# Agent attention with a squared-ReLU network on one Trainium2 core: the first batch's passes over 98 columns instead of 49, its small work in another order

## The chip, the cores and the metric

One Trainium2 chip, of which the kernel uses one core. A core has five engines with a queue each: PE (TensorE, the matrix unit), DVE (VectorE), ACT (ScalarE), POOL (GpSimd) and SP (SyncE), which here only starts transfers (DMAs). PE reads SBUF and writes PSUM. The metric is the device time of one execution in microseconds (us), lower is better; a kernel's time is the median of its runs.

## What is computed

Four batches of 12480 tokens with 128 channels, 49 agents per batch, and a two-layer network behind the attention:

```python
scale = 1.0 / np.sqrt(q.shape[-1])
def sm(a, b):
    s = scale * (a @ b.transpose(0, 2, 1))
    s = s - s.max(-1, keepdims=True)
    e = np.exp(s)
    return e / (e.sum(-1, keepdims=True) + 1e-09)
agent_v = sm(agents, k) @ v          # 49 x 128 per batch
attn = sm(q, agents) @ agent_v       # 12480 x 128 per batch
h = np.maximum(attn @ w_in, 0.0)     # d_ff = 2048
out = h * h @ w_out
```

The two weight matrices arrive in 64-bit floats; the kernel turns their bits into f32 numbers itself ("decode").

## The kernel before

The kernel doesn't form the attention's output. Per batch it forms `agent_v` (transposed: avT), multiplies it with w_in into a table aw of 49 rows and 2048 columns, and the first layer is then the softmaxed queries (49 wide) times that table. High and low parts keep the precision: aw_hi and aw_ex for the table, w and x for the queries.

**The first batch** is computed alone, ahead of everything else, with an order written out by hand: while `alone[0]` is true every instruction of an engine is issued behind the one before it in program order (`Ordered`, `queued`, lines 55 to 74). Its stages:

- *Keys.* 13 blocks, twelve of 1024 tokens (8 tiles of 128) and one of 192. `scores` (177) multiplies each tile, as the stationary operand, with the agents (49 columns moving) into a PSUM buffer h; ACT copies the scores to s, DVE takes the running maximum mx. An f32 matmul is two records ("passes") in the trace. In between, `make_w_in` (143) decodes parts of w_in: ACT forms t from raw, DVE runs five operations on t and rest (`decoded`, 124), POOL adds them into win.
- *Maximum.* `maxima` (195): m on DVE, a transpose on PE, its maximum, a diagonal dg, and a matmul with ones that broadcasts it, copied to mb.
- *Values.* Per block `whole_exps` (227): subtract mb (DVE and POOL take turns), exponential on ACT in place in s. `whole_values` (233): each tile of values, stationary, times 49 columns of s, all accumulated in one PSUM bank; POOL adds the exponentials into mx for the row sums. In between, `make_w_out` (147) decodes parts of w_out (t, wo_hi, wo_lo), and the first 960 queries are softmaxed step by step (`queries`, 326).
- *Sums and tables.* `whole_sums` (248): the row sums e1, their reciprocal rl and avT. `tables` (301): four matmuls win x avT of 512 columns; ACT writes aw_hi, DVE aw_lo (3 buffers), SP moves pieces of aw_lo into aw_hi and aw_ex.

**The feed-forward part** then runs over 52 groups of 960 queries, each 16 steps k of two halves j (loop at 517). `first` (376) makes h from w, x and the table; `hidden` (394): ACT relu r, DVE r times h (gg), ACT square g_hi, DVE or POOL the rest g_lo; `second` (419) multiplies with wo_hi and wo_lo into o, four steps later. PE, ACT and DVE keep program order there too. Beside it `queries` prepares the next group (started at c = 0, one step from c = 2 on), and `background` the next batch's keys, values and tables; both share one PSUM bank, psa. None of it is issued ahead of the first batch's last instruction on SP, ACT, DVE and POOL (`behind`).

PSUM buffers h: 3 (two banks each). Buffers of loaded keys and values in the first batch: 11; of raw weights: 8.

Of the kernel before, what the change touches and what calls it, by code (L numbers as in the profile page):

```python
# [9 lines left out]
F32 = mybir.dt.float32  # L10
# [4 lines left out]
AX = mybir.AxisListType  # L15
PSUM = bass.MemoryType.PSUM

P = 128
# [18 lines left out]
def agent_attention_relu2(ctx: ExitStack, tc: tile.TileContext, qT, kT, v, agT, w_in, w_out, outT):  # L37
    nc = tc.nc
    C, NTOK = qT.shape
    _, B, NA = agT.shape  # L40
# [21 lines left out]
    alone = [True]  # L62
# [11 lines left out]
    pe, act, dve, pool, sync = (Ordered(e) for e in (nc.tensor, nc.scalar, nc.vector, nc.gpsimd, nc.sync))  # L74
# [4 lines left out]
    small = ctx.enter_context(tc.tile_pool(name="small", bufs=1))  # L79
# [6 lines left out]
    ag = const.tile([C, B, NA], F32, name="ag")  # L86
# [75 lines left out]
    state = {}  # L162
# [7 lines left out]
    def load_values(b, i, pool, name):  # L170
        at, rows, nt = blocks[i]
        vt = pool.tile([P, KB], F32, name=name).rearrange("p (t c) -> p t c", c=C)
        src = v[b, at : at + rows * nt, :].rearrange("(p t) c -> p t c", p=rows)
        sync.dma_start(vt[:rows, :nt, :], src)
        return vt

    def scores(b, i, kt):
        st = state.setdefault(b, {"s": []})
        _, rows, nt = blocks[i]
        ps = bank()  # L180
        sv = ps[:rows, : nt * NA].rearrange("p (t a) -> p t a", a=NA)
        for t in range(nt):
            pe.matmul(sv[:, t, :], kt[:, t * rows : (t + 1) * rows], ag[:, b, :], start=True, stop=True)  # L183
        yield
        s = sp.tile([P, NT, NA], F32, name="s")
        act.copy(s[:rows, :nt, :], sv)
        if i == 0:
            st["mx"] = small.tile([P, NT, NA], F32, name="mx")
            dve.tensor_copy(st["mx"], sv)
        else:  # L190
            mx = st["mx"][:rows, :nt, :]
            dve.tensor_max(mx, mx, sv)
        st["s"].append(s)

    def maxima(b):
        st = state[b]
# [30 lines left out]
    def whole_exps(b, i, eng):  # L227
        _, rows, nt = blocks[i]
        e = state[b]["s"][i][:rows, :nt, :]
        less_maximum(b, i, e, eng)  # L230
        act.activation(e, e, AF.Exp, scale=scale)

    def whole_values(b, i, vt):
        st = state[b]
        _, rows, nt = blocks[i]
        e = st["s"][i][:rows, :nt, :]
        if i == 0:
            st["pv"] = bank()
        for t in range(nt):
            pe.matmul(  # L240
                st["pv"][:C, :NA], vt[:rows, t, :], e[:, t, :],
                start=(i == 0 and t == 0), stop=(i == NK - 1 and t == nt - 1),
            )
        if i > 0:
            es = st["mx"][:rows, :nt, :]
            pool.tensor_add(es, es if i > 1 else st["s"][0], e)

    def whole_sums(b):
        st = state[b]
        e1 = small.tile([P, 2, NA], F32, name="e1")  # L250
        for n in range(2):
            dve.reduce_sum(e1[:, n, :], st["mx"].rearrange("p t a -> p a t"), axis=AX.X)
        pz = bank()
        pe.matmul(pz[:K2, :1], e1.rearrange("p h a -> p (h a)"), ones[:, :1], start=True, stop=True)
        rl = st["rl"] = small.tile([K2, 1], F32, name="rl")
        dve.tensor_scalar_add(rl, pz[:K2, :1], 1e-9)
        dve.reciprocal(rl, rl)
        av = st["avT"] = small.tile([C, K2], F32, name="avT")
        act.copy(av[:, :NA], st["pv"][:C, :NA])
        dve.tensor_copy(av[:, NA:], st["pv"][:C, :NA])  # L260

    def values(b, i, vt):
        st = state[b]
# [37 lines left out]
    def tables(b):  # L301
        st = state[b]
        rl, av = st["rl"], st["avT"]
        hi = st["hi"] = aw.tile([P, FF], F32R, name="aw_hi")
        ex = st["lo"] = aw.tile([P, NCH // NQ, P], F32R, name="aw_ex")
        for n in range(FF // 512):
            yield
            cs = slice(n * 512, (n + 1) * 512)
            pw = bank()
            pe.matmul(pw[:K2, :], av, win[:, cs], start=True, stop=True)  # L310
            yield
            act.activation(hi[:K2, cs], pw[:K2, :], AF.Copy, scale=rl)
# [151 lines left out]
    def run(gen):  # L464
        for _ in gen:
            pass
# [6 lines left out]
        pe.matmul(idle[:, 0, :P], ones, ones, start=True, stop=True)  # L473

    with tc.tile_pool(name="pre", bufs=PRE) as pre, tc.tile_pool(name="dec", bufs=2) as dec:
        raws = {}
        kts, vts = [], []
        early = {i: i - 3 for i in range(3, 8)} | {9: 5, 11: 6}
        for i in range(NK):
            kts.append(load_keys(0, i, pre, "ahead"))  # L480
            if 1 <= i <= NW:
                raws[i - 1] = ask_w_in(dec, i - 1)
            if i == NK - 3:
                q0 = queries(0)
                next(q0)
            run(scores(0, i, kts[i]))
            if i in early:
                make_w_in(dec, early[i], raws.pop(early[i]))
        top = maxima(0)
        next(top)  # L490
        next(top)
        next(q0)
        run(top)
        for i in range(NK):
            if i == NW:
                make_w_in(dec, NW - 1, raws.pop(NW - 1))
            vts.append(load_values(0, i, pre, "ahead"))
            if 1 <= i <= NW:
                raws[NW + i - 1] = ask_w_out(dec, i - 1)
        for i in range(2):  # L500
            whole_exps(0, i, (pool, dve)[i % 2])
        for i in range(NK):
            if i + 2 < NK:
                whole_exps(0, i + 2, (pool, dve)[i % 2])
            whole_values(0, i, vts[i])
            next(q0, None)
            if 3 <= i < NW + 3:
                make_w_out(dec, i - 3, raws.pop(NW + i - 3))
        run(q0)
        whole_sums(0)  # L510
        run(tables(0))
    behind = [chain[eng] for eng in (nc.sync, nc.scalar, nc.vector, nc.gpsimd)]

    alone[0] = False
    ffn = ctx.enter_context(tc.tile_pool(name="ffn", bufs=4))
    todo = ahead = iter(())
    for k in range(total + LAG):
        if k < total:
            g, c = divmod(k, SLOTS)
            b, i = divmod(g, NB)  # L520
            if i == 0 and c == 0 and b + 1 < B:
                todo = background(b + 1)
                done = 0
            goal = (i * SLOTS + c + 1) * STEPS / (SPREAD * NB * SLOTS)
            while done < goal and step(todo):
                done += 1
            if c == 0 and g + 1 < B * NB:
                ahead = queries(g + 1)
                step(ahead)
            if c >= 2:  # L530
                step(ahead)
        if k % 2 == 0:
            hs = first(k) if k < total else ()
            if hs:
                hidden(k, hs[0])
            for n in range(2):
                if k + n >= LAG:
                    second(k + n - LAG)
            copied_out()
            if hs:  # L540
                hidden(k + 1, hs[1])
# [35 lines left out]
```

## Time and profile before

| | us |
|---|---|
| median of 3 runs | 2089.64 (2088.23 to 2092.76) |
| the profiled execution | 2089.47 |
| its span from first to last instruction | 2087.6 |
| warm-up matmuls, from the span's start | 0 to 6.13 |
| key matmuls | 6.13 to 43.45 |
| maximum | 43.45 to 55.59 |
| value matmuls | 55.59 to 102.00 |
| sums | 102.00 to 108.76 |
| table matmuls | 108.76 to 114.68 |

The page's first part, busy time and share of the span for each engine:

```profile
PE 2051.5 (98%) x10932; PEld 1621.5 (78%) x10932; DVE 1672.7 (80%) x1835; ACT 1775.2 (85%) x2100; POOL 1275.1 (61%) x1110
```

PE is busy 98% of the span, and PEld is its weight load, which overlaps. A busy PE need not be a fast one: the granted clock has a row of its own. A row of the timeline reads: start, length, engine, line, operation, out<-in, shapes, count, and in brackets the idle time before it with what ended it. L58 is the helper through which all ordered instructions go, so rows are told apart by their tiles. "ahead" are the loaded keys or values.

### The profile page before, as it was taken

To read this page: it belongs to the slowest core of one execution; us is meant where nothing else is said; L and a number is where in the kernel's file an instruction comes from. 1 tells how busy PE (TensorE), PEld (TensorE's weight loads), DVE (VectorE), ACT (ScalarE), POOL (GpSimd) and SP (SyncE) were. 2 spreads that over 40 slices of the span, in tenths; PEclk is the share of its full clock that TensorE was granted. 3 is DMA by queue.
4 is the path that set the end of the run, shared out by engine and by line. 5 is a ranking of instruction groups with operands and counts; after the bars stand their busy time and mean duration, and the time that the engine had idled before them with its cause. 6 is when DMAs were issued, how large, how long until landed. Compare 5 with 4: busy or idle time off the path is not lost. (4 is left out here: it accounts for less than half of the span.)

```text
span 2087.6 us, 31676 instructions
## 1 busy us (share of the span) xinstructions
PE 2051.5 (98%) x10932; PEld 1621.5 (78%) x10932; DVE 1672.7 (80%) x1835; ACT 1775.2 (85%) x2100; POOL 1275.1 (61%) x1110
## 2 busy tenths in 40 slices
PE   8889999999999999999999999999999999999999
PEld 8857777777778877777778877777777777777777
DVE  3465888889887788888887788888888888888887
ACT  1265899989888899999898889999889999989897
POOL 1643587766554477776555458777556565656565
PEclk6588999999999999999999999999999999999999
DMA  8132222121112212221112211221111111111100
GB/s 300 46 118 87 70 75 75 52 65 63 53 56 79 65 53 80 63 60 61 63 40 71 88 35 60 68 75 41 44 51 35 46 35 47 35 47 35 38 23 20
DMA packets 55943, 131.34 MB, mean 63 GB/s; under 512 B 6712, under 2 KB 35336, under 8 KB 55784
## 3 DMA queue, kind: packets, MB, share of 16 engines
q1 hardware_dynamic: 55784, 129.33, 19.3%
q8 instruction: 87, 1.43, 0.3%
q14 instruction: 72, 0.59, 0.1%
HBM read 80.97 MB, written 25.56 MB: 51 GB/s over the span
## 5 line engine op out<-in xcount | busy, mean ns | idle before, releaser
L407 POOL TENSOR_TENSOR g_lo<-gg,g_hi 128x480 fp32r<-128x480 f32 x832 | 999.1, 1222 | 711.2 <-DVE gg L58 457.5
L58 ACT ACTIVATE r<-h 128x960 f32<-128x960 f32 x832 | 800.7, 962 | 145.5 <-PE h L58 132.7
L58 ACT ACTIVATE g_hi<-r 128x960 fp32r<-128x960 f32 x832 | 837.5, 1007 | 34.8 <-PE o L58 1.0
L58 DVE TENSOR_TENSOR h<-r,h 128x960 f32<-128x960 f32 x416 | 482.5, 1160 | 156.7 <-ACT r L58 151.6
L58 DVE TENSOR_TENSOR gg<-r,h 128x960 f32<-128x960 f32 x416 | 478.0, 1149 | 85.4 <-ACT r L58 79.9
L58 PE MATMUL o<-g_hi,wo_hi 128*128 128x480 f32 x1664 | 539.2, 405 | 0.0
L58 DVE TENSOR_TENSOR g_lo<-h,g_hi 128x960 fp32r<-128x960 f32 x416 | 481.0, 1156 | 48.3 <-ACT g_hi L58 7.7
L58 PE MATMUL h<-w,aw_hi 128*128 128x480 f32 x1664 | 485.4, 398 | 10.7 <-DVE gg L58 7.7
L58 PE MATMUL o<-g_hi,wo_lo 128*128 128x480 f32 x1664 | 495.4, 379 | 0.0
L58 PE MATMUL o<-g_lo,wo_hi 128*128 128x480 f32 x1664 | 494.7, 378 | 0.0
L58 PEld LDWEIGHTS o<-g_hi,wo_hi 128*128 128x128 f32 x1664 | 280.9, 188 | 117.4 <-issue 69.5
L58 PEld LDWEIGHTS o<-g_hi,wo_lo 128*128 128x128 f32 x1664 | 313.3, 188 | 47.2
L58 PEld LDWEIGHTS o<-g_lo,wo_hi 128*128 128x128 f32 x1664 | 313.3, 188 | 46.7
L58 PEld LDWEIGHTS h<-w,aw_hi 128*128 128x128 f32 x1664 | 289.3, 190 | 59.3 <-DVE gg L58 20.3
L58 PE MATMUL h<-x,aw_ex 19*128 19x480 f32 x1664 | 207.9, 481 | 1.3 <-DMA x<-w 1.0
L58 PEld LDWEIGHTS h<-x,aw_ex 19*128 19x128 f32 x1664 | 81.6, 182 | 142.4 <-issue 138.1
L334 PEld LDWEIGHTS psa<-ag,qt 128*120 128x120 f32 x816 | 100.6, 184 | 6.5 <-issue 0.7
L58 DVE COPY ob<-o 128x480 f32<-128x480 f32 x104 | 68.2, 656 | 35.9 <-PE o L58 35.5
L334 PE MATMUL psa<-ag,qt 128*120 128x49 f32 x816 | 95.9, 261 | 0.0
L219 POOL TENSOR_TENSOR vs<-vt,vs 128x1024 fp32r<-128x1024 f32 (+1 forms) x39 | 81.6, 2094 | 12.6 <-ACT vs L217 12.3
L183 PEld LDWEIGHTS psa<-ag,kt 128*128 128x128 f32 (+1 forms) x588 | 76.4, 195 | 3.6
L183 PE MATMUL psa<-ag,kt 128*128 128x49 f32 (+1 forms) x588 | 72.7, 271 | 0.0
(112 smaller groups left out, 1069.0 us busy)
## 6 DMA issues: line engine op xcount, KB each, us to landing
qt<-in_qT SPq DMA_DIRECT2D x52, 480.0 KB
out_T<-ob SPq DMA_DIRECT2D x104, 240.0 KB
kt<-in_kT SPq DMA_DIRECT2D x36, 512.0 KB
vt<-in_v SPq DMA_DIRECT2D x36, 512.0 KB
x<-w SPq DMA_DIRECT2D x416, 35.6 KB
ahead<-in_kT SPq DMA_DIRECT2D x12, 512.0 KB
ahead<-in_v SPq DMA_DIRECT2D x12, 512.0 KB
w<-w SPq DMA_DIRECT2D x104, 56.2 KB
```

The source lines that it names most:

```text
L58: ins = issue(*args, **kw)
L183: pe.matmul(sv[:, t, :], kt[:, t * rows : (t + 1) * rows], ag[:, b, :], start=True, stop=True)
L219: eng.tensor_sub(out[:, :, n : n + w], x, out[:, :, :w].bitcast(F32))
L334: pe.matmul(sv[:, t, :], qt[:, t * TP : (t + 1) * TP], ag[:, b, :], start=True, stop=True)
L407: nc.gpsimd.tensor_sub(lo[:, n, :], gg[:, n, :], hi[:, n, :].bitcast(F32))
```

## The change

In the first batch, key and value matmuls move 98 columns. For keys these are the agents of batches 0 and 1 side by side, of which only the first 49 columns of the result are read (each result tile now takes 128 columns, four to a bank, in both banks of an h buffer). For values, the exponentials of two neighbouring tiles are moved together past each value tile; even tiles go to one bank and odd ones to the other, the matching 49 columns of both are added at the end. The other changes are of order:

- DVE's maximum comes ahead of ACT's copy of the same scores.
- The input weight parts are decoded behind key blocks 3, 4, 6, 7, 9, 10 and the first two value blocks; output parts 0 to 5 behind value blocks 3, 4, 6, 7, 9, 10; output parts 6 and 7 behind the tables.
- The queries' scores go ahead of the maximum's transpose; four matmuls of ones (`warm`) stand ahead of the broadcast.
- All subtractions are on DVE, three ahead; POOL's additions are issued ahead of the matmuls (`add_weights`); e1 is summed once and copied, ahead of the last value block.
- Values are loaded interleaved with the output weights, later ones between the value matmuls.
- The second group's queries start ahead of the tables, with their scores and first steps right behind, and go on at every step of the first group.

```diff
     def scores(b, i, kt):
...
+        if alone[0]:
+            h = ps_h.tile([P, 2, 512], F32, name="h")[:rows, :, :].rearrange("p h (t x) -> p h t x", x=P)
+            n = nt // 2
+            for t in range(nt):
+                out = h[:, t // n, t % n, : 2 * NA]
+                keys = kt[:, t * rows : (t + 1) * rows]
+                pe.matmul(out, keys, ag[:, :2, :].rearrange("c b a -> c (b a)"), start=True, stop=True)
+            sv = h[:, :, :n, :NA]
...
         yield
         s = sp.tile([P, NT, NA], F32, name="s")
-        act.copy(s[:rows, :nt, :], sv)
...
         if i == 0:
-            st["mx"] = small.tile([P, NT, NA], F32, name="mx")
-            dve.tensor_copy(st["mx"], sv)
+            dve.tensor_copy(mx, sv)
         else:
             dve.tensor_max(mx, mx, sv)
+        act.copy(s, sv)
...
         if i == 0:
-            st["pv"] = bank()
+            st["pv"] = ps_h.tile([P, 2, 512], F32, name="h")
         for t in range(nt):
+            pair = e[:, t - t % 2 : t - t % 2 + 2, :].rearrange("p t a -> p (t a)")
             pe.matmul(
-                st["pv"][:C, :NA], vt[:rows, t, :], e[:, t, :],
-                start=(i == 0 and t == 0), stop=(i == NK - 1 and t == nt - 1),
+                st["pv"][:C, t % 2, : 2 * NA], vt[:rows, t, :], pair,
+                start=(i == 0 and t < 2), stop=(i == NK - 1 and t >= nt - 2),
             )
+    def add_weights(b, i):
...
+            pool.tensor_add(es, es if i > 1 else st["s"][0], st["s"][i][:rows, :nt, :])
 
     def whole_sums(b):
...
-        for n in range(2):
-            dve.reduce_sum(e1[:, n, :], st["mx"].rearrange("p t a -> p a t"), axis=AX.X)
+        dve.reduce_sum(e1[:, 0, :], st["mx"].rearrange("p t a -> p a t"), axis=AX.X)
+        dve.tensor_copy(e1[:, 1, :], e1[:, 0, :])
+        yield
+        av = st["avT"] = small.tile([C, K2], F32, name="avT")
+        act.copy(av[:, :NA], st["pv"][:C, 0, :NA])
+        dve.tensor_add(av[:, :NA], av[:, :NA], st["pv"][:C, 1, NA : 2 * NA])
+        dve.tensor_copy(av[:, NA:], av[:, :NA])
...
+        def warm(n):
+            idle = bank()
+            for _ in range(n):
+                pe.matmul(idle[:, :P], ones, ones, start=True, stop=True)
...
+        between = {i: n for n, i in enumerate((3, 4, 6, 7, 9, 10))}
...
         top = maxima(0)
         next(top)
+        next(q0)
         next(top)
-        next(q0)
+        warm(2)
+        next(top)
+        warm(2)
         run(top)
+        for i in range(3):
+            whole_exps(0, i, dve)
+        for i in range(2):
+            add_weights(0, i)
+        between = {i: n for n, i in enumerate((0, 1, 3, 4, 6, 7, 9, 10))}
         for i in range(NK):
+            if i + 3 < NK:
+                whole_exps(0, i + 3, dve)
             if i + 2 < NK:
-                whole_exps(0, i + 2, (pool, dve)[i % 2])
+                add_weights(0, i + 2)
+            if i == NK - 1:
+                ends = whole_sums(0)
+                next(ends)
             whole_values(0, i, vts[i])
             next(q0, None)
...
         run(q0)
-        whole_sums(0)
+        run(ends)
+        ahead = queries(1)
+        next(ahead)
         run(tables(0))
+        next(ahead)
+        next(ahead)
+        for n in range(NW - 2, NW):
+            make_w_out(dec, n, raws.pop(NW + n))
...
-            if c == 0 and g + 1 < B * NB:
+            if c == 0 and 0 < g < B * NB - 1:
                 ahead = queries(g + 1)
                 step(ahead)
-            if c >= 2:
+            if c >= 2 or g == 0:
                 step(ahead)
```

What the change moves is seen in the order of the instructions on an engine. ACT's queue in the key stage, from the third key block on; "COPY s" copies a block's scores, "ACTIVATE t" is the first step of a decode. Before:

```order
L58 COPY s<-h 128x392 [waits PE_49] x4
L58 ACTIVATE t<-raw 128x256 [waits DMAHW3_49]
L58 COPY s<-h 128x392 [waits PE_49]
L58 ACTIVATE t<-raw 128x256 [waits DMAHW5_49]
L58 COPY s<-h 128x392 [waits PE_49]
```

And now:

```order
L58 COPY s<-h 128x392 [waits DVE_49] x4
L58 ACTIVATE t<-raw 128x256 [waits DMAHW3_49]
L58 COPY s<-h 128x392 [waits DVE_49]
L58 ACTIVATE t<-raw 128x256 [waits DMAHW5_49]
L58 COPY s<-h 128x392 [waits DVE_49] x2
```

The copy waits for DVE (its maximum of the same block) where it waited for PE, and t still stands behind the copy.

DVE's queue between the tables (aw_lo) and the first products of the feed-forward part (gg). Before:

```order
L58 TENSOR_REDUCE e_727<-mx 128x49 x2
L58 TENSOR_SCALAR rl<-h 98x1
L58 RECIPROCAL rl<-rl 98x1
L58 COPY avT<-h 128x49
L58 SCALAR_TENSOR_TENSOR aw_lo<-h,rl,aw_hi 49x512 x4
L58 TENSOR_TENSOR gg<-r,h 128x960
```

And now, where m, e and z belong to the second group's queries:

```order
L58 SCALAR_TENSOR_TENSOR aw_lo<-h,rl,aw_hi 49x512 x4
L58 TENSOR_REDUCE m<-h 120x8
L58 TENSOR_TENSOR e<-h,m 120x392
L58 TENSOR_SCALAR t<-t 128x256 x2
L58 SCALAR_TENSOR_TENSOR t<-raw,t 128x256
L58 TENSOR_SCALAR rest<-t 128x256
L58 SCALAR_TENSOR_TENSOR rest<-raw,rest 128x256
...
L362 TENSOR_REDUCE z<-e 120x8
L363 TENSOR_SCALAR z<-z 120x8
L364 RECIPROCAL z<-z 120x8
L58 TENSOR_TENSOR gg<-r,h 128x960
```

Two decodes (one of them is the "...") and the second queries' first steps came in between.

PE's queue where the second group begins; w_999 (now w_904) are that group's weights, "psa<-identr,pp" the transposes that make them. Before:

```order
L183 MATMUL psa<-ag,kt 128x49 x8
L356 MATMUL psa<-identr,pp 98x120 x8
L58 MATMUL h<-w_999,aw_hi 128x480 x4
L183 MATMUL psa<-ag,kt 128x49 x8
L58 MATMUL h<-x_1000,aw_ex 128x480 x4
```

And now:

```order
L374 MATMUL psa<-identr,pp 98x120 x4
L58 MATMUL h<-w_629,aw_hi 128x480 x2
L58 MATMUL h<-x_630,aw_ex 128x480 x4
...
L58 MATMUL h<-w_904,aw_hi 128x480 x2
L191 MATMUL psa<-ag,kt 128x49 x8
L58 MATMUL h<-w_904,aw_hi 128x480 x2
L58 MATMUL h<-x_905,aw_ex 128x480 x4
```

The second half of the transposes now stands in the first group (w_629), two pairs of steps ahead of its use, and the first half two pairs earlier, where all of them stood directly ahead of their use.

More of the change, by code (lines that the diff above doesn't have):

```diff
@@ L179, in scores @@
         _, rows, nt = blocks[i]
[L180 to L183, printed above, removed]
+        if alone[0]:
[6 more added lines that the diff above has]
+            sv = h[:, :, :n, :NA]
+        else:
+            sv = bank()[:rows, : nt * NA].rearrange("p (t a) -> p t a", a=NA)
+            for t in range(nt):
+                pe.matmul(sv[:, t, :], kt[:, t * rows : (t + 1) * rows], ag[:, b, :], start=True, stop=True)
         yield
         s = sp.tile([P, NT, NA], F32, name="s")
-        act.copy(s[:rows, :nt, :], sv)
+        st["s"].append(s)
         if i == 0:
             st["mx"] = small.tile([P, NT, NA], F32, name="mx")
-            dve.tensor_copy(st["mx"], sv)
+        s, mx = (x[:rows, :nt, :] for x in (s, st["mx"]))
+        if alone[0]:
+            s, mx = (x.rearrange("p (h t) a -> p h t a", h=2) for x in (s, mx))
+        if i == 0:
+            dve.tensor_copy(mx, sv)
         else:
-            mx = st["mx"][:rows, :nt, :]
             dve.tensor_max(mx, mx, sv)
-        st["s"].append(s)
+        act.copy(s, sv)
     def maxima(b):
@@ L237, in whole_values @@
         if i == 0:
-            st["pv"] = bank()
+            st["pv"] = ps_h.tile([P, 2, 512], F32, name="h")
         for t in range(nt):
+            pair = e[:, t - t % 2 : t - t % 2 + 2, :].rearrange("p t a -> p (t a)")
             pe.matmul(
-                st["pv"][:C, :NA], vt[:rows, t, :], e[:, t, :],
-                start=(i == 0 and t == 0), stop=(i == NK - 1 and t == nt - 1),
-            )
+                st["pv"][:C, t % 2, : 2 * NA], vt[:rows, t, :], pair,
+                start=(i == 0 and t < 2), stop=(i == NK - 1 and t >= nt - 2),
+            )
+    def add_weights(b, i):
+        st = state[b]
+        _, rows, nt = blocks[i]
         if i > 0:
             es = st["mx"][:rows, :nt, :]
-            pool.tensor_add(es, es if i > 1 else st["s"][0], e)
+            pool.tensor_add(es, es if i > 1 else st["s"][0], st["s"][i][:rows, :nt, :])
     def whole_sums(b):
@@ L257, in whole_sums @@
         dve.reciprocal(rl, rl)
-        av = st["avT"] = small.tile([C, K2], F32, name="avT")
-        act.copy(av[:, :NA], st["pv"][:C, :NA])
-        dve.tensor_copy(av[:, NA:], st["pv"][:C, :NA])
     def values(b, i, vt):
@@ L475, in agent_attention_relu2, with next_values @@
     with tc.tile_pool(name="pre", bufs=PRE) as pre, tc.tile_pool(name="dec", bufs=2) as dec:
+        def warm(n):
+            idle = bank()
+            for _ in range(n):
+                pe.matmul(idle[:, :P], ones, ones, start=True, stop=True)
         raws = {}
         kts, vts = [], []
-        early = {i: i - 3 for i in range(3, 8)} | {9: 5, 11: 6}
+        def next_values():
+            vts.append(load_values(0, len(vts), pre, "ahead"))
+        between = {i: n for n, i in enumerate((3, 4, 6, 7, 9, 10))}
         for i in range(NK):
@@ L486, in agent_attention_relu2 @@
             run(scores(0, i, kts[i]))
-            if i in early:
-                make_w_in(dec, early[i], raws.pop(early[i]))
+            if i in between:
+                make_w_in(dec, between[i], raws.pop(between[i]))
+        next_values()
+        for n in range(6):
+            next_values()
+            raws[NW + n] = ask_w_out(dec, n)
         top = maxima(0)
         next(top)
+        next(q0)
         next(top)
-        next(q0)
+        warm(2)
+        next(top)
+        warm(2)
         run(top)
-        for i in range(NK):
[L495 to L502, printed above, removed]
+        for i in range(3):
[3 more added lines that the diff above has]
+        between = {i: n for n, i in enumerate((0, 1, 3, 4, 6, 7, 9, 10))}
+        for i in range(NK):
+            if i + 3 < NK:
+                whole_exps(0, i + 3, dve)
             if i + 2 < NK:
-                whole_exps(0, i + 2, (pool, dve)[i % 2])
+                add_weights(0, i + 2)
+            if i == NK - 1:
+                ends = whole_sums(0)
+                next(ends)
             whole_values(0, i, vts[i])
             next(q0, None)
-            if 3 <= i < NW + 3:
-                make_w_out(dec, i - 3, raws.pop(NW + i - 3))
+            if i in between:
+                n = between[i]
+                if n < 2:
+                    make_w_in(dec, NW - 2 + n, raws.pop(NW - 2 + n))
+                    next_values()
+                    raws[2 * NW - 2 + n] = ask_w_out(dec, NW - 2 + n)
+                else:
+                    make_w_out(dec, n - 2, raws.pop(NW + n - 2))
+            if i >= 2 and len(vts) < NK:
+                next_values()
         run(q0)
-        whole_sums(0)
+        run(ends)
+        ahead = queries(1)
+        next(ahead)
         run(tables(0))
+        next(ahead)
+        next(ahead)
+        for n in range(NW - 2, NW):
+            make_w_out(dec, n, raws.pop(NW + n))
     behind = [chain[eng] for eng in (nc.sync, nc.scalar, nc.vector, nc.gpsimd)]
@@ L515, in agent_attention_relu2 @@
     ffn = ctx.enter_context(tc.tile_pool(name="ffn", bufs=4))
-    todo = ahead = iter(())
+    todo = iter(())
     for k in range(total + LAG):
```

## The prediction

> **What bounds the kernel now.** I read the stages first, then the TensorE clock, then the engines inside each stage. The page's row of granted clock, in tenths over 40 slices of 52 us, says where to look:
>
> ```profile
> PEclk6588999999999999999999999999999999999999
> ```
>
> Next the span in stages (start:end and length in us, then for each engine busy us and records, the granted clock, DMA share and GB/s):
>
> ```profile
> 6.13:43.45 37.32, 37.31 (x198) 37.15 (x196) 16.14 (x42) 7.92 (x19) 4.34 (x6) 0.56 0.96 364
> 43.45:55.59 12.14, 4.12 (x19) 3.90 (x20) 7.82 (x20) 1.24 (x5) 3.23 (x4) 0.50 0.30 104
> 55.59:102.00 46.41, 44.09 (x204) 43.45 (x204) 19.03 (x44) 13.24 (x31) 27.89 (x32) 0.50 0.12 42
> 102.00:108.76 6.76, 0.46 (x3) 0.41 (x3) 3.10 (x8) 0.51 (x2) 2.93 (x4) 0.50 0.00 0
> ...
> 114.68:178.17 63.49, 55.69 (x262) 42.55 (x263) 35.82 (x40) 40.75 (x48) 27.53 (x22) 0.81 0.38 122
> 178.17:2087.60 1909.43, 1898.80 (x10211) 1486.90 (x10209) 1589.19 (x1681) 1707.86 (x1992) 1207.43 (x1029) 1.00 0.18 55
> ```
>
> From 178 us on PE is busy 1898.80 of 1909.43 us at full clock, on the same work before and after, so what is saved ahead of it comes off the end. Ahead of it lie key scores, maximum, value passes, sums, tables and the start of the feed-forward part. In the key and value stages PE is never free, yet at half clock. A value pass (one of the two that an f32 matmul takes) costs 44.09 / 204 = 0.216 us.
>
> Why half clock? PE alone, in short windows and in windows 3.41 us long (the clock changes on that grid):
>
> ```profile
> 1.40:3.53 2.13, 2.13 (x12) 1.00 0.79 184
> 12.00:14.13 2.13, 2.13 (x12) 0.50 1.03 411
> 4.30:6.00 1.70, 1.70 (x17) 1.00 0.97 348
> 7.50:9.20 1.70, 1.70 (x18) 1.00 0.95 354
> ...
> 10.92:14.33 3.41, 3.41 (x18) 0.50 1.03 406
> 109.91:113.32 3.41, 3.41 (x6) 0.50 0.00 0
> 120.15:123.56 3.41, 2.75 (x7) 0.50 0.11 29
> 123.56:126.97 3.41, 3.41 (x11) 0.50 0.12 30
> 133.80:137.21 3.41, 1.85 (x12) 1.00 0.49 172
> ```
>
> The first and third windows hold warm-up passes that move 128 columns, the second and fourth key passes that move 49. At one clock both come at one rate (12 records in 2.13 us; 17 and 18 in 1.70), so the weight load sets the pace and up to 128 columns hide behind it. (The first window reads 1.00 because the first clock record comes later; its rate is that of half clock.) With 49 columns the clock fell at 10.92 after one whole window of them and never rose while PE was busy without a break. It rose after the windows full of long passes (109.91, 123.56). So what counts is how much PE moves, not whether it is occupied.
>
> ```profile
> 108.76 5.92 PE L58 MATMUL h<-win,avT 128*98 128x512 f32 x8 [0.56 <-DVE avT L58]
> ```
>
> Eight passes of 512 columns take 4.56 us at half clock (to 113.32) and 1.36 at full, 7.28 / 8 = 0.91 us at half: 1.8 ns a column. 49 columns then fill 0.087 us, 40% of a pass; 98 fill 0.174, 80%, still under 0.216. 40% lets the clock fall and doesn't raise it; a window with PE busy 1.85 of 3.41 us (133.80, 54%) held it.
>
> [...]
>
> **The change, part by part.** *Keys.* At full clock a block's 16 passes take half of 16 x 0.216, 1.7 us, so PE no longer bounds. VectorE does, since the copy and the weight decode are queued otherwise:
>
> ```profile
> 15.53 0.49 ACT L58 COPY s<-h 128x392 f32<-128x392 f32 x1 [2.93 <-PE h L58]
> 15.91 0.43 ACT L58 ACTIVATE t<-raw 128x256 f32<-128x256 f32 x1
> ```
>
> ```profile
> 16.05 0.56 DVE L58 TENSOR_TENSOR mx<-mx,h 128x392 f32<-128x392 f32 x1 [2.85 <-ACT s L58]
> 16.53 0.61 DVE L58 TENSOR_SCALAR t<-t 128x256 f32<-128x256 f32 x2
> ...
> 17.96 0.43 DVE L58 SCALAR_TENSOR_TENSOR rest<-raw,rest 128x256 f32<-128x256 uint32 x1
> ```
>
> Before, copy s, then the maximum beside the decode's first step t (on ACT), then the decode, 16.53 to 18.39 = 1.86. Now copy s waits for the maximum and t stands behind it: 0.56 + 0.38 + 0.43 + 1.86 = 3.2 us of VectorE a block, with 0.95 of waiting, over the 1.7 of PE. Block 3 is scored at 6.13 + 4 x 1.75 = 13.1; six decode blocks at 3.2 and four others at 0.48 end at 34.2. The row maximum follows:
>
> ```profile
> 45.90 0.82 DVE L58 TENSOR_REDUCE m<-mx 128x49 f32<-128x392 f32 x1
> ...
> 51.03 0.21 DVE L58 COPY mb<-h 128x49 f32<-128x49 f32 x1 [3.14 <-PE h L58]
> ```
>
> ```profile
> 46.86 0.42 PE L58 MATMUL h<-ident,m 128*49 128x128 f32 x1 [3.42 <-DVE m L58]
> ...
> 50.33 0.66 PE L58 MATMUL h<-dg,ones 49*128 49x49 f32 x2
> ```
>
> m ends at 35.0 instead of 46.72. PE has by then been idle for more than a window, so I count half clock: transpose 0.5, eight warm passes 1.7 (ahead of the broadcast; they cover its small VectorE work), broadcast 0.7, mb 0.25: 38.2. The queries' scores, which stood between transpose and broadcast, are now ahead of both, hidden by VectorE. The input decode that stood between mb and the first subtraction is later. A subtraction and an exponential (rows below, 0.6 to 0.9 and 0.53) lead to the first value pass: 39.5 instead of 55.59, **-16.1**.
>
> *Values.* PE has 196 passes (42.3 us at half clock, 21.2 at full) and eight transposes at about half of that each. The others now run ahead of it. VectorE gets all thirteen subtractions:
>
> ```profile
> L58 DVE TENSOR_TENSOR s<-s,mb 128x392 f32<-128x392 f32 x6 | 5.3, 876 | 0.0
> L58 DVE TENSOR_REDUCE e<-mx 128x49 f32<-128x392 f32 x2 | 1.5, 804 | 2.8 <-POOL mx L58 2.8
> L58 DVE TENSOR_SCALAR z<-z 120x8 f32<-120x8 f32 x1 | 0.8, 847 | 0.0
> L58 DVE TENSOR_REDUCE m<-h 120x8 f32<-120x392 f32 x1 | 0.6, 559 | 0.0
> ```
>
> ```profile
> L58 ACT ACTIVATE s<-s 128x392 f32<-128x392 f32 x12 | 6.1, 527 | 25.0 <-POOL s L58 19.7 <-DVE s L58 5.3
> ...
> L58 POOL TENSOR_TENSOR e<-e,z 120x392 f32<-120x392 f32 x1 | 1.0, 987 | 0.4 <-DVE z L58 0.4
> ```
>
> 12 x 0.876 + 0.25, eight decodes at 1.86, the queries' five operations 2.7 (three like m, z, a reciprocal the size of mb), the sum 0.80 and its copy 0.2: 29.4 us. Each decode again waits for a t that ACT issues behind an exponential, 0.53 + 0.43 less an overlap, 0.9 x 8 = 7.2. From 38.2 that ends at 74.8. POOL's adds now come ahead of PE, so of the 6.76 us of sums a copy, an add and a copy are left, some 0.9 (three like mb, with their waits): table matmuls start at **75.7** if PE keeps up. At half clock throughout, PE ends at 39.5 + 43.1 = 82.6 and they start at **83.5**; before, 108.76.
>
> Does the clock, once down, rise at 80%? The nearest windows differ in short passes over 19 rows:
>
> ```profile
> 120.01 1.43 PE L58 MATMUL h<-x,aw_ex 19*128 19x480 f32 x4
> ...
> 124.22 0.77 PE L58 MATMUL h<-x,aw_ex 19*128 19x480 f32 x4
> ```
>
> Without these, 123.56 raised it at 3.41 - 0.7 = 2.7 us (80%) and 120.15 failed at 2.75 - 1.3 = 1.45 (42%); with them, 120.15 failed at 81%. Passes over 19 of 128 rows should count for little, so I take the rise, and keep the other as a rival. With the rise PE needs 22 us, two waits at half clock of some 5 us each and a hole for the queries' transposes, so VectorE ends last or equal.
>
> *Behind the tables.* Two output decodes and the second queries stand between aw_lo and the first relu product:
>
> ```profile
> 117.51 0.74 DVE L58 SCALAR_TENSOR_TENSOR aw_lo<-h,rl,aw_hi 49x512 fp32r<-49x512 f32 x1 [2.19 <-DMA aw_ex<-aw_lo]
> ```
>
> ```profile
> 117.68 1.01 ACT L58 ACTIVATE g_hi<-r 128x960 fp32r<-128x960 f32 x1
> 118.59 0.95 ACT L58 ACTIVATE r<-h 128x960 f32<-128x960 f32 x1
> ```
>
> The fourth aw_lo waits for a DMA until 8.75 us after the tables begin. Behind it: 0.74, m and e 1.1, two decodes 3.7, to 14.3; z and its reciprocal 1.2 (less or more with its add), POOL's multiply 1.0, to 16.5. ACT meanwhile reaches the first r at some 14.5, but ahead of its square stands the cast pp, which waits for that multiply: cast 0.5, square 1.0, and the second r starts 18.0 after the tables begin, against 118.59 - 108.76 = 9.83: **+8.2**. Nothing hides it; PE waits for h buffers. SP's second-query transfer goes ahead of the tables' and is hidden by their matmuls.
>
> *Second queries.* In exchange, this goes:
>
> ```profile
> 161.21 0.89 PE L356 MATMUL psa<-identr,pp 120*98 120x120 f32 x4 [1.51 <-DVE mx L192]
> ...
> 165.00 1.97 PE L58 MATMUL h<-w,aw_hi 128*128 128x480 f32 x4 [1.34 <-DMA w<-w]
> ```
>
> ```profile
> 161.11:178.17 17.06, 14.20 (x46) 11.60 (x47) 2.99 (x4) 5.44 (x7) 2.37 (x2) 0.50 0.25 81
> ```
>
> PE ran out at 159.70 because the transposes stood directly ahead of the matmuls that need them, and worked at half clock to 178.17: 18.47 us for what takes 14.20 / 2 = 7.1 at full. They now stand many matmuls earlier: **-11.4**, if nothing else is late there; the next may be VectorE's maximum of the new keys, worth 1.5 once.
>
> Sum from the profiled execution, 2089.47 (median 2089.64): 75.7 - 108.76 = -33.1, +8.2, -11.4: -36.3, **2053**.
>
> **Rivals.** *Clock stays at half in the values*: 83.5 in place of 75.7, **2061**. For it, the 120.15 window; against, the 123.56 one. *The clock doesn't follow columns at all* (the change doesn't do what it says): keys end at 43.4 as before, the queries' scores add 3.3 behind them (16 x 0.21), values take 43 us from 51.4, tables begin at 95.4: -13.4 + 8.2 - 11.4, **2073**; against, PE less busy (54%) held at 133.80 what 49 columns without a break lost at 10.92. [...] *The stall at the second queries stays* behind a later wait: 2053 + 11.4, **2064**. *Slower*: if 98 columns did not hide behind the weight load, 392 passes would each take up to 0.174 more, +68 and **2121**; it turns slower from 0.10 us a pass on (40.5 / 392). Against: 128 columns cost no more than 49 in the windows above.
>
> **How the numbers follow.** Forecast 0.46, half clock 0.33, stall stays 0.08, clock not by columns 0.08, slower 0.02, better than forecast (no lag in the keys, 6 x 0.95 = 5.7 less, 2047) 0.03. The range goes from 2044 (that, and the warm passes at full clock) to 2067 (the stall, with some microseconds of other waits); it leaves out the two that end above. About 0.2% (4 us) is what a measurement of this kernel can tell; every case but the last rival is faster by more.
>
> **What would show it.** Granted clock 1.00 from 4 to about 30 us in the keys; VectorE waiting for ACT t in each decode there; value passes at 0.11 us with VectorE or POOL ending last (forecast), or 196 at 0.21 without a gap (half clock); tables beginning near 76 or 84; second r some 18 us after that; no hole ahead of the second queries. Wrong would be a steady stage longer than 1909, or passes over 0.22 us.

## The result, and the profile after

| | before | after |
|---|---|---|
| median, us | 2089.34 (2088.23 to 2092.76, 4 runs) | 2055.54 (2055.20 to 2055.71, 4 runs) |
| the profiled execution | 2089.47 | 2055.71 |
| its span | 2087.6 | 2053.9 |

The ratio is 0.9835, with a 95% interval of 0.9818 to 0.9852: the change takes 33.8 us away. On the page of the changed kernel, the engines' row and the row of granted clock:

```profile
PE 2015.8 (98%) x10940; PEld 1587.0 (77%) x10940; DVE 1681.4 (82%) x1843; ACT 1769.1 (86%) x2100; POOL 1270.6 (62%) x1103
...
PEclk9799999999999999999999999999999999999999
```

PE's share is 98% as before. What changed is the clock at the left end: 9 and 7 tenths where the page of before has 6, 5 and twice 8. The changed kernel's span in stages (start:end and length, busy us and records of PE, PEld, DVE, ACT and POOL, clock, DMA share, GB/s):

```profile
6.67:34.47 27.80, 24.42 (x214) 23.73 (x212) 15.83 (x41) 7.34 (x17) 3.62 (x5) 1.00 1.03 396
34.47:40.85 6.38, 2.73 (x12) 2.37 (x12) 3.83 (x10) 1.21 (x4) 0.73 (x1) 0.61 0.99 365
40.85:79.84 38.99, 28.34 (x206) 27.87 (x207) 30.25 (x60) 12.91 (x31) 26.25 (x28) 0.81 0.29 96
...
85.41:144.01 58.60, 49.44 (x263) 38.94 (x262) 39.83 (x48) 40.42 (x51) 28.67 (x25) 0.83 0.38 125
144.01:2053.90 1909.89, 1899.66 (x10211) 1486.23 (x10209) 1589.73 (x1682) 1703.62 (x1994) 1209.54 (x1031) 1.00 0.17 55
```

The last stage holds 10211 PE records in 1909.89 us, where before held 10211 in 1909.43: nothing of the difference lies there. In the value stage no engine is full any more (PE 28.34, DVE 30.25, POOL 26.25 of 38.99 us): they wait for one another. PE's timeline of the changed kernel at the places that decide:

```profile
36.60 0.42 PE L58 MATMUL h<-ident,m 128*49 128x128 f32 x1 [2.13 <-DVE m L58]
...
40.85 13.49 PE L58 MATMUL h<-s,ahead 128*128 128x98 f32 x96 [1.53 <-ACT s L58]
58.65 0.92 PE L58 MATMUL h<-identr,pp 120*98 120x120 f32 x4 [4.32 <-POOL pp L58]
...
79.84 5.57 PE L58 MATMUL h<-win,avT 128*98 128x512 f32 x8
...
106.75 1.17 PE L58 MATMUL o<-g_hi,wo_hi 128*128 128x480 f32 x2
```

The value passes begin at 40.85 instead of 55.59, the tables at 79.84 instead of 108.76, and the first output matmul runs at 106.75 instead of 124.92. So 28.9 us are won up to the tables and only 18.2 are left one stage later. When the first output matmul of step k starts in the two traces, and how much earlier:

```
k             0       10       12       14      104      831
before   124.92   155.12   172.79   181.13   403.12  2081.90
after    106.75   135.21   141.07   146.95   368.96  2048.36
        -18.17   -19.92   -31.72   -34.18   -34.16   -33.54
```

Between k = 10 and 14 another 14.3 us come off (26.01 us before, 11.74 after): the hole at the second queries is gone. From there on the distance stays.

### The profile page after: what moved, and what is told of

Read it like the earlier page. It is cut to its first block, busy times and chain, and to the rows that moved or that the text cites. A ratio compares the mean times of both kernels' runs of the same rounds, so it can differ in the third digit from the quotient of the medians.

```text
span 2053.9 us, 31686 instructions
## 1 busy us (share of the span) xinstructions
PE 2015.8 (98%) x10940; PEld 1587.0 (77%) x10940; DVE 1681.4 (82%) x1843; ACT 1769.1 (86%) x2100; POOL 1270.6 (62%) x1103
## 3 DMA queue, kind: packets, MB, share of 16 engines
q1 hardware_dynamic: 55784, 129.33, 19.3%
```

## The experiments

Each kernel was timed once, beside the kernel before (2088.69 to 2092.30 us on the chips used); only e9 has four runs. Where a kernel computes a part differently, its expectation or the text says so. "Offset" is the difference to before in the table's sense at k = 104.

### Does the clock follow the columns? (e1, e2, e3, e6)

e1 is the changed kernel with 49 columns in keys and values; e2 has 98 in the keys and 49 in the values; e3 moves 74 in the values.

```diff
 e1 (keys), e1 and e2 (values)
-                out = h[:, t // n, t % n, : 2 * NA]
+                out = h[:, t // n, t % n, :NA]
...
-                pe.matmul(out, keys, ag[:, :2, :].rearrange("c b a -> c (b a)"), start=True, stop=True)
+                pe.matmul(out, keys, ag[:, 0, :], start=True, stop=True)
...
+            at = t % 2 * NA
...
-                st["pv"][:C, t % 2, : 2 * NA], vt[:rows, t, :], pair,
+                st["pv"][:C, t % 2, at : at + NA], vt[:rows, t, :], e[:, t, :],
 e3 (values)
+            at = t % 2 * (2 * NA - 74)
...
+                st["pv"][:C, t % 2, at : at + 74], vt[:rows, t, :], pair[:, at : at + 74],
```

> The changed kernel with 49 columns again in key and value passes, all else as changed. Theory (the clock follows the columns moved): granted clock 0.50 from some 11 us through the values; key blocks every 3.4 us, end near 44, first value pass near 52, 196 passes of 0.216 and the transposes to 95.6, table matmuls at 96.5 instead of 79.84, so 2055.5 + 16.7 = 2072. Rival (the clock follows occupation, or the order of the small work alone made the gain): clock and time as with 98 columns, 2055.5.

> The changed kernel with 49 columns in the value passes only. Theory: clock down at 36 us as before and never up in the values; 196 passes of 0.216 us plus transposes from 40.9 to 84.7, tables at 85.6 instead of 79.84, so 2061. The gain of 98 columns in the values is then only about 6 us, because VectorE (which ended at 79.7 in the changed kernel) stands close behind. Rival (values are bound by VectorE whatever the clock): 2055.5.

> The changed kernel with 74 columns in the value passes (0.13 of 0.216 us, 61% of a pass instead of 80%). Tells where the clock's rise lies: if 61% is enough, clock 1.00 from some 46 us and 2055.5; if not, as with 49 columns, 0.50 through the values and about 2061.

Measured: e1 2069.81, e2 2059.24, e3 2061.18 us. PE alone by windows (busy, records, clock), of e1 over its keys and its values, then of e2, then of e3:

```profile
7.30:43.40 36.10, 36.10 (x187) 0.55 0.91 345
50.69:94.92 44.23, 43.64 (x207) 0.50 0.25 83
```

```profile
6.00:33.00 27.00, 24.04 (x208) 1.00 1.03 395
40.20:84.43 44.23, 43.64 (x206) 0.50 0.25 88
```

```profile
41.50:85.71 44.21, 43.58 (x206) 0.50 0.25 84
```

e1 goes the way of the theory that columns set the clock: it differs from the changed kernel in nothing but the columns, and its time is 14.3 us longer. With 49 columns PE is busy 43.64 of 44.23 us and the clock stays at 0.50; 74 columns do the same at the same pace, and 98 raise it. Read narrowly, in windows 3.41 us long of the changed kernel:

```profile
42.76:46.18 3.42, 3.42 (x18) 0.50 0.00 0
46.18:49.59 3.41, 3.41 (x32) 1.00 0.66 231
...
53.00:56.42 3.42, 1.34 (x12) 1.00 0.81 292
...
32.52:35.94 3.42, 1.88 (x16) 1.00 1.05 384
```

Eighteen passes of 98 columns in one window, and the next is at full clock (42.76). A window with PE busy 1.34 of 3.42 us (39%) ended it (53.00). So did the one at 32.52 with the queries' scores, sixteen passes of 49 columns: PE was busy 1.88 us (55%) there, while 1.85 us of passes over 480 columns held the clock in the kernel before (133.80 in the prediction). By this pair, holding the clock goes by the columns moved as well.

By the prediction's 1.8 ns a column, 74 columns fill 0.133 of 0.216 us, 62%, and 98 fill 80%: the clock rises somewhere between. In the value stages of e1 and e2 an occupied PE (43.64 of 44.23 us) did not raise the clock from 0.50.

e3 is 1.9 us above e2 though its value stage is no longer: its keys began at 7.27 instead of 6.03, behind 32 warm-up matmuls that took 6.45 us instead of 5.20, and its tables took 6.7 us instead of 6.0. The columns are worth most in the keys: e1 and e2, which differ there alone, are 10.6 us apart, while half clock in the values costs 3.7 us (e2 against the changed kernel).

e6 is the kernel before with the 98-column matmuls alone, all order as before.

> The kernel before with 98 columns in key and value passes and nothing else changed. Theory (columns alone): clock 1.00 in the keys, which then follow VectorE and the transfers and end near 30; first value pass near 41; the values are then bound by POOL, which had 27.9 us of work there plus waits, to some 75; sums still take 6.8 behind it, tables at 82, start and hole as before: 2089 - 27 = 2062. Rival (without the new order of the small work 98 columns bring little, as POOL and VectorE run in the matmuls' wake): 2075 or more.

Measured 2071.47, offset -18.3: neither the 2062 of the columns' theory nor the rival. In PE's timeline of e6 the value passes now run out of exponentials:

```profile
64.09 3.63 PE L58 MATMUL h<-s,ahead 128*128 128x98 f32 x16 [3.26 <-ACT s L58]
...
73.63 2.99 PE L58 MATMUL h<-s,ahead 128*128 128x98 f32 x16 [3.57 <-ACT s L58]
...
90.44 5.89 PE L58 MATMUL h<-win,avT 128*98 128x512 f32 x8 [0.87 <-DVE avT L58]
```

The tables begin at 90.44, 18.3 us earlier than before, and the hole at the second queries stays whole. So the columns alone are worth 18.3 us in the old order (e6) and 13.9 in the new one (offset of e1 -20.3 against -34.2); the order alone is worth 20.3 (e1), of which the hole is most.

### What did VectorE wait for in the keys? (e4, e7)

e4 puts ACT's copy of the scores ahead of DVE's maximum again; e7 leaves it behind, but issues ACT's t of a decode ahead of that copy, and in the values ahead of the exponential.

```diff
 e4
+        act.copy(s, sv)
         if i == 0:
...
-        act.copy(s, sv)
 e7
+    def begun(dec, raw):
+        t = dec.tile([P, WCH], U32, name="t")
+        act.activation(t.bitcast(F32), raw[:, :, 1].bitcast(F32), AF.Abs)
+        return raw, t
...
+            if i in between:
+                raws[between[i]] = begun(dec, raws[between[i]])
             run(scores(0, i, kts[i]))
```

> The changed kernel with ACT's copy of the scores ahead of DVE's maximum again. Theory (each decode in the keys cost 0.95 us of waiting, 6 x 0.95 = 5.7): DVE's decodes follow the maximum without a wait, the row maximum m ends near 31 instead of 36.5, and since VectorE bounds the values too, some 5 us come off: 2050 to 2051. Rival (the maximum first starts 0.5 us earlier per block and helps; the lag is hidden elsewhere): 2055.5 or slower.

> The changed kernel with ACT's first decode step t issued ahead of the score copy (keys) and ahead of the exponential (values) that it stood behind. Theory (VectorE bounds both stages, and waits 0.95 us in each of six decodes there and 0.9 to 1.7 in each of eight here): about 5.5 off in the keys and 5 to 7 in the values, where POOL's share then limits it: 2043 to 2046. Rival (the values are bound by POOL): only the keys' 5.5, 2050.

Measured: e4 2050.15, offset -39.3; e7 2048.76, offset -41.3. The wait, in DVE's timeline of the changed kernel, first in the keys and then in the values:

```profile
15.44 0.62 DVE L58 TENSOR_SCALAR t<-t 128x256 f32<-128x256 f32 x2 [0.89 <-ACT t L58]
...
57.14 1.61 DVE L58 TENSOR_SCALAR t<-t 128x256 f32<-128x256 f32 x2 [1.05 <-ACT t L58]
```

PE's timeline of e7, where the maximum's transpose stood at 36.60 in the changed kernel:

```profile
32.59 0.28 PE L58 MATMUL h<-ident,m 128*49 128x128 f32 x1 [0.98 <-DVE m L58]
35.84 13.79 PE L58 MATMUL h<-s,ahead 128*128 128x98 f32 x96 [1.52 <-ACT s L58]
52.96 0.92 PE L58 MATMUL h<-identr,pp 120*98 120x120 f32 x4 [3.33 <-POOL pp L58]
...
73.21 6.69 PE L58 MATMUL h<-win,avT 128*98 128x512 f32 x8
```

The first value pass comes 5.0 us earlier (4.0 in e4), the tables 6.6 (4.0 in e4); 0.5 of it in e7 is the earlier start of its keys (6.21 instead of 6.67). Six waits of 0.89 are 5.3 us: the one order "maximum before copy" costs about the 5.7 that the prediction said of it. In the values the same step is worth only 6.6 - 5.0 = 1.6 of the 7.2 that were counted for eight waits. The waits do go there, from 7.3 us ahead of t<-t in the changed kernel to 0.7 in e7. But the decodes' forty operations then take 23.5 us instead of 18.2, as here, in DVE's timeline of e7, the pair that took 0.62 in the keys of the changed kernel:

```profile
65.39 1.83 DVE L58 TENSOR_SCALAR t<-t 128x256 f32<-128x256 f32 x2 [0.28 <-ACT t L58]
```

What DVE no longer waits for ACT, it loses in longer operations. In the changed kernel such operations had POOL at work beside them (rows in the last section); that it is so in e7 too is an estimate from those. e7 misses its 2043 to 2046 by that.

### What do the parts behind the tables cost, and what do they buy? (e5, e8 to e11)

e5 is the changed kernel with the second queries issued as before the change, step by step inside the feed-forward part. e8 is e7 with the two last output parts decoded behind steps 4 and 6, and the second queries started in the first steps; only their transfer stays ahead of the tables.

```diff
 e5
-        ahead = queries(1)
-        next(ahead)
         run(tables(0))
-        next(ahead)
-        next(ahead)
...
-            if c == 0 and 0 < g < B * NB - 1:
+            if c == 0 and g + 1 < B * NB:
...
-            if c >= 2 or g == 0:
+            if c >= 2:
 e8 (against e7)
         run(tables(0))
-        next(ahead)
-        next(ahead)
-        for n in range(NW - 2, NW):
-            make_w_out(dec, n, raws.pop(NW + n))
...
+            if k in (4, 6):
+                alone[0] = True
+                make_w_out(ffn, NW - 4 + k // 2, raws.pop(2 * NW - 4 + k // 2))
+                alone[0] = False
```

> The changed kernel with the second group's queries started in the first group again, from step 2 on, as before the change. Theory: the hole ahead of the second group (14.3 us between the two kernels, from the tenth to the fourteenth step) comes back, and the start of the feed-forward part is some 4 us earlier, since m, e, z and the cast pp no longer stand ahead of the first relu: 2055.5 + 14.3 - 4 = 2066. Rival (the hole came from the slow start of the old kernel and stays away, or another wait fills the place): 2051 to 2055.

> As t_early, and the output parts 6 and 7 decoded behind steps 4 and 6 of the feed-forward part, the second queries' first steps in its steps 0 and 1 instead of ahead of it (six instead of eight buffers for raw weights, and two more that stay). Theory: the 10.75 us by which the start came later than before (from tables to the first output matmul) go, less some 2 for the decodes between the products: 2035 to 2038. Rival (VectorE and ACT then fall behind in the first steps and PE waits there instead): 2043 to 2046, as t_early.

Measured: e5 2079.30, e8 2071.49 us. Both miss by far, on the same side. At k = 0 e8 stands at -34.2, 9.4 us ahead of e7, but by k = 104 at -18.7; e5 goes from -17.4 to -10.4. e5's start is no shorter than the changed kernel's (26.8 us from the tables to the first output matmul, 26.9 there), and at k = 22 it stands 7.2 us behind it, half of the 14.3 that were said; the rest is lost later. What PE waited for in the changed kernel, in e5 and in e8 from 130 to 260 us (us in total, times, longest):

```profile
PE h L58 <- DMA x<-w: 0.2, 1, 0.2
```

```profile
PE h L58 <- DMA x<-w: 10.6, 11, 1.4
```

```profile
PE h L58 <- DMA x<-w: 10.2, 10, 1.7
```

x is the low part of a group's query weights: PE transposes the weights, ACT copies them to w, SP moves pieces of w into w and x. So PE waits not at the second queries alone, but again at those of the third and fourth group, whose lines of code are the same in all these kernels. I counted in each trace the matmul records between the last transpose of a group's first half and the first matmul that reads its x, and compared what was lost between k = 22 and 104:

```
         records (us) ahead, groups 1, 2, 3            offset at k = 22, 104    lost
before   25 ( 8.5)    63 (11.0)   49 (9.7)
after   135 (22.7)    63 (11.0)   49 (9.7)             -34.2     -34.2          0.0
e5       27 ( 6.1)    39 ( 6.5)   27 (5.9)             -27.0     -10.4         16.7
e8       21 ( 5.6)    39 ( 6.5)   27 (5.9)             -35.0     -18.7         16.3
```

From this came a theory, the distance: moving the decodes or the second queries shifts where the scheduler (which orders the instructions that no hand-written order ties down, when the kernel is built) puts the later groups' transposes among PE's matmuls, and 27 or 39 records are too few. Three kernels test it. e9 and e10 are e8 with two steps of the second queries ahead of the loop again; in e9 the decodes stand behind steps 6 and 8, in e10 behind 4 and 6. e11 is the changed kernel with output parts 6 and 7 decoded ahead of the last value block.

```diff
 e9 and e10 (against e8)
         run(tables(0))
+        next(ahead)
+        next(ahead)
 e9 (against e10)
-            if k in (4, 6):
+            if k in (6, 8):
 e11 (against the changed kernel)
+            if i == NK - 2:
+                for n in range(NW - 2, NW):
+                    make_w_out(dec, n, raws.pop(NW + n))
...
-        for n in range(NW - 2, NW):
-            make_w_out(dec, n, raws.pop(NW + n))
```

> As in e8 (output parts 6 and 7 decoded inside the feed-forward part), but the two decodes stand behind steps 6 and 8 instead of 4 and 6, and two more steps of the second queries stand ahead of the feed-forward part. In the order of TensorE's instructions the last transposes of the weights of groups 1, 2 and 3 then stand 91, 55 and 48 matmuls ahead of the first one that reads their copy x (in e8 13, 31 and 27; in the changed kernel 111, 55 and 48). Theory of the distance (later groups lost time in e5 and e8 because the transposes stood too few matmuls ahead, so that TensorE waited for the DMAs x<-w and its clock fell): no waits for x<-w after the start, the start's gain of e8 (about 9 us against e7) stays, less what the decodes take from DVE and POOL later: 2038 to 2044 us. Rival (it is the decodes beside the feed-forward part that cost, by DVE and POOL): holes again near 190 and 240 us, 2060 to 2072 us.

> The same as e9 but with the two decodes behind steps 4 and 6. Distances of the transposes for groups 1, 2, 3: 83, 31 and 27 matmuls. Theory of the distance: no hole in group 1, but TensorE waits for x<-w at the starts of groups 2 and 3 as in e5 and e8, which cost some 16 us there from step 22 to the settled offset: 2054 to 2060 us. Rival (decodes two steps earlier change nothing that lasts): within 2 us of e9.

> The changed kernel with output parts 6 and 7 decoded ahead of the first batch's last values instead of behind the tables; the second queries stay where the change put them. Tables later by the DVE and POOL work of two parts that then stands ahead of them (up to 2 x 2.8 us), first step's start after the tables shorter by 4 to 8 us. By the start alone 2050 to 2057 us. But the distances for groups 1, 2, 3 are 83, 31 and 27 matmuls: the theory of the distance adds the loss of groups 2 and 3, some 16 us: 2064 to 2073 us.

(The expectations count a matmul once where the trace can hold two records of it; 55 there is 63 in the table, 31 is 39.) Measured: e9 2046.83 us (2045.38 to 2047.21, 4 runs; ratio to before 0.9793, 0.9776 to 0.9809), e10 2062.10, e11 2069.10.

```
         records (us) ahead, groups 1, 2, 3            offset at k = 22, 104    lost
e9      115 (22.0)    63 (11.0)   49 (9.7)             -42.6     -42.6          0.1
e10      99 (16.8)    39 ( 6.5)   27 (5.9)             -42.5     -27.8         14.7
e11      99 (16.8)    39 ( 6.5)   27 (5.9)             -35.7     -20.5         15.2
```

e9 and e10 stand within 0.1 us of each other at k = 22, and end 15.3 us apart. How it is lost, at the third group in e10, from PE's timeline and SP's:

```profile
171.03 0.48 PE L379 MATMUL psa<-identr,pp 120*98 120x120 f32 x4
...
177.78 0.48 PE L58 MATMUL h<-x,aw_ex 19*128 19x480 f32 x1
178.63 0.48 PE L58 MATMUL h<-x,aw_ex 19*128 19x480 f32 x1 [0.38 <-DMA x<-w]
180.60 0.76 PE L58 MATMUL h<-x,aw_ex 19*128 19x480 f32 x1 [1.49 <-DMA x<-w]
182.69 0.76 PE L58 MATMUL h<-x,aw_ex 19*128 19x480 f32 x1 [1.33 <-DMA x<-w]
```

```profile
172.61 0.86 SPq L387 DMA_DIRECT2D w<-w  x1
173.53 2.45 SPq L389 DMA_DIRECT2D x<-w  x4
```

The four pieces of x are issued one after another until 175.98, and the last lets its matmul go at 182.69, 11.3 us after the transposes gave way to the next matmul (at 171.34). A distance of 11.0 us just covers that, one of 6.5 does not. The waits are 3.2 us in all; they also take the clock (e10, PE by windows), so that 6.4 us are gone at k = 28:

```profile
178.72:182.13 3.41, 1.15 (x2) 0.65 0.32 124
182.13:185.54 3.41, 2.85 (x6) 0.50 0.03 11
```

In e9 the same four matmuls, from transposes to x, run in one piece:

```profile
165.05 0.48 PE L379 MATMUL psa<-identr,pp 120*98 120x120 f32 x4
...
176.26 0.94 PE L58 MATMUL h<-x,aw_ex 19*128 19x480 f32 x4
```

The theory's numbers hold for e10's and e11's loss (14.7 and 15.2 where 16 was said, e11 within its range); e10's total misses its 2054 to 2060, and e9 its 2038 to 2044, by about the same 2 to 3 us. That part goes with the decodes inside the loop: e9's first output matmul runs 6.8 us ahead of e7's (93.35 against 100.11) and by k = 10 only 1.3 are left, most of it lost between k = 6 and 8, 9.2 us instead of 4.5 (e9, PE):

```profile
111.53:120.74 9.21, 8.23 (x44) 0.83 0.32 99
```

Sixteen key passes lie in this stretch that e7 has elsewhere. Besides, the late parts are needed at once, and PE waits 0.27 us for wo_hi and 0.17 for wo_lo, then 0.54 for a copy of scores, and part of the stretch runs at half clock. What each of these costs was not separated.

e9 is the fastest kernel here. Its gain over the changed kernel, 8.7 us, is mostly e7's edit (offset -41.3 against -42.6).

## Why the prediction came true, step by step

The forecast was 2053, and the time is 2055.5, inside the forecast's own case: the clock rises in both stages, the hole goes, the start pays. That only 2.5 us are missing is partly luck: two terms came 6.7 us short and another 4.6 over. Its terms:

- **Clock by columns.** Shown by e1 to e3, the rise at 80% as taken. The fall while PE stands idle ahead of the maximum came too (clock 0.61 from 34.47 to 40.85). The prediction counted it from "more than a window" of idling; here PE stood idle for 2.13 us, to 36.60, and the clock fell to 0.50 at 35.94. Ahead of the tables PE was idle for 5.32 us, to 79.51, and it fell at 76.90. What the rise in the values is worth was put too high: 7.8 us (83.5 against 75.7), while e2 without it is 3.7 slower, since VectorE ends close behind. So it is the clock's rows, more than the time, that tell the forecast from its rival at half clock.
- **Keys, -16.1; measured 55.59 - 40.85 = -14.7.** The mechanism, VectorE waiting for t behind the copy, is shown by e4 and e7. What was late is the row maximum, in DVE's timeline of the changed kernel:

```profile
35.64 0.82 DVE L58 TENSOR_REDUCE m<-mx 128x49 f32<-128x392 f32 x1
```

  It ends at 36.46, not 35.0; 0.5 of that is the stage's own later start (first key pass at 6.67, not 6.13). From m to the first value pass it took 4.4 us, 4.5 predicted.
- **Values and tables, -33.1; measured -28.9.** 1.4 of the missing 4.2 us come from the keys. The rest is a step mis-sized: "12 x 0.876 + 0.25, eight decodes at 1.86 ... 29.4 us" took the decode's 1.86 from a key block, a stage with POOL busy 4.34 of 37.32 us. Here both are busy at once: DVE's pair t<-t takes 1.61 us at 57.14 where it took 0.62 in the keys, and the eight decodes, each from its first operation to its last, 19.3 us instead of 14.9. The waits ahead of them came as counted, 7.3 for 7.2. PE's wait of 4.32 us for POOL's pp also brought a second stretch at half clock (56.42 to 63.24); it was named as "a hole for the queries' transposes" but not priced. What that stretch alone cost was not tried; at the stage's end it is PE that waits for DVE.
- **Start of the feed-forward part, +8.2; measured +9.2 at the second r, +10.7 at the first output matmul.** ACT's timeline of the changed kernel:

```profile
96.33 0.97 ACT L58 ACTIVATE r<-h 128x960 f32<-128x960 f32 x1 [1.33 <-POOL wo_lo L58]
97.58 0.52 ACT L228 CAST pp<-e 120x392 fp32r<-120x392 f32 x1 [0.28 <-POOL e L365]
98.01 1.00 ACT L58 ACTIVATE g_hi<-r 128x960 fp32r<-128x960 f32 x1
98.91 0.95 ACT L58 ACTIVATE r<-h 128x960 f32<-128x960 f32 x1
```

  The second r stands 98.91 - 79.84 = 19.1 after the tables begin (18.0 predicted, with the cast pp ahead of the square as described). The step that was off is the first r, "at some 14.5": it starts at 16.5 and waits for POOL's last wo_lo, which the sum had left out. From the tables' beginning to the first output matmul it takes 26.9 us with decodes and queries, 26.8 without the queries (e5), 19.8 without the decodes (e11) and 16.5 without either (e8; before 16.2): the decodes set this start, and the queries lie beside them.
- **Hole at the second queries, -11.4; measured -14.3, and -1.7 more from k = 0 to 10.** Mechanism right (135 records ahead instead of 25), size too small. PE between the first output matmuls of k = 10 and 14, of before in three stretches, and after:

```profile
155.12:159.70 4.58, 4.57 (x32) 1.00 0.38 114
159.70:178.17 18.47, 14.20 (x46) 0.54 0.26 78
178.17:181.13 2.96, 2.96 (x25) 1.00 0.02 10
```

```profile
135.21:146.95 11.74, 11.74 (x76) 1.00 0.28 92
```

  The step "14.20 / 2 = 7.1 at full" counted all 46 records of the hole as work that stays there. Of the 103 records of these four steps only 76 are left in the changed kernel; the others run elsewhere now, and the steps from 0 to 10 are none the longer for it. "If nothing else is late there" was the condition, and it holds in the changed kernel by little: in e5 to e11 it turns on 39 or 63 records.
- **The sum** was -36.3; the terms measured are -28.9 + 10.7 - 1.7 - 14.3 = -34.2, and +0.4 in the long stage. 4.2 and 2.5 us less gained than forecast, and 4.6 more at the queries.

What the prediction did not see at all is that the work ahead of the loop also sets the later groups' distances: e8 takes the start's price of some 10 us away and gets the holes of three groups, while e9 takes 7 of it away (20.0 us from the tables to the first output matmul) and gets none.

Left open: why the scheduler puts the same lines of later groups 63 or 39 records ahead. The orders show that it does so, and e9 and e10 that moving two decodes by two steps decides it; its reasons were not tried.

## What to carry to other kernels

A matmul whose weight load takes longer than its columns should be given more columns, even useless ones, where PE is the bound and its clock is down: what counted here is the share of the pass that moves data, and 80% raised the clock where 62% did not. Once PE is twice as fast, look for the wait between two small engines that takes its place; here one instruction's place in ACT's queue cost some 5 us. And when work is moved ahead of a loop that a scheduler orders, compare the distance from producer to consumer in the later rounds too, in us against the chain between them (11.3 here): an edit ahead of the loop can be paid for, or earned, there.

## What the runs showed of the hardware

DVE slowed beside POOL in certain operations only. DVE's and POOL's timelines of the changed kernel, behind the tables:

```profile
90.28 0.61 DVE L58 TENSOR_SCALAR t<-t 128x256 f32<-128x256 f32 x2
...
92.16 1.51 DVE L58 TENSOR_SCALAR t<-t 128x256 f32<-128x256 f32 x2
```

```profile
91.86 0.85 POOL L58 TENSOR_TENSOR t<-t,wo_hi 128x256 f32<-128x256 f32 x1 [12.55 <-ACT wo_hi L58]
92.80 0.72 POOL L58 TENSOR_TENSOR wo_lo<-t,rest 128x256 fp32r<-128x256 f32 x1
```

With POOL idle the pair takes 0.61 us; begun while POOL works it takes 1.51 and ends at 93.67, just after POOL's second operation (93.52). The subtraction s<-s,mb took 0.56 us where POOL began only after it (45.21, POOL at 45.37) and 1.09 begun beside it (55.00, POOL from 54.81). The step e<-h,m, whose h is a PSUM buffer, took 0.57 us at 42.11, with POOL at work from 41.35 to 43.57, and 0.56 at 89.80 with POOL idle. Why some operations are slowed and others not was not shown.

The clock's grid of 3.41 us does not lie alike in every execution. It changed at 10.92, 113.32, 120.15, 126.97, 161.11 and 178.17 us in the kernel before, and at 35.94, 46.18, 56.42, 63.24, 76.90 and 83.72 in the changed one: within each trace these lie whole steps of 3.41 apart, between the two 1.13 beside a whole step. With the same instructions ahead of them the keys began at 6.03 us in e2 and at 7.50 in e5, behind warm-up matmuls of 5.20 and 6.68 us, which is 1.5 us of noise in any single run here.
